# Layer 1 of a four-layer kernel: tiles 8 to 15 turned by crossbar DMA transposes, and the keys' map in one VectorE operation

## The chip, the cores and the metric

The kernel runs on one core of a Trainium2 chip. A core has five engines that work side by side, each through its own list of instructions in order: TensorE (PE in the profile; its weight loads, PEld, overlap its matmuls), VectorE (DVE), ScalarE (ACT), GpSimd (POOL) and SyncE (SP), which here issues the DMAs. An instruction that has to wait holds up all that stand behind it in its engine's list. The metric is the device time of one run in microseconds (us); less is better.

## The reference, cut to what matters

The input `A_x` has 2048 tokens (S) of 576 numbers (D). Four layers follow each other: linear attention, MLP, attention, MLP, with the same weights in both pairs. Each adds its result to x.

```python
def _A_ref(x, wqkv, wo):            # H = 32 heads of 18
    q, k, v = ...                   # (x @ wqkv), split by head
    phi = lambda t: jnp.where(t > 0, t + 1, jnp.exp(t)) + 1e-6
    pq, pk = phi(q), phi(k)
    kv = jnp.einsum("bhsd,bhse->bhde", pk, v)
    z = jnp.einsum("bhsd->bhd", pk)
    num = jnp.einsum("bhqd,bhde->bhqe", pq, kv)
    den = jnp.einsum("bhqd,bhd->bhq", pq, z)[..., None] + 1e-6
    return (num / den) @ wo         # heads joined again
def _B_ref(x, w1, b1, w2, b2):      # 576 -> 4608 -> 576
    h = _gelu(_layernorm(x) @ w1 + b1)
    return h @ w2 + b2
x = x + _A_ref(_layernorm(x), ...); x = x + _B_ref(x, ...)   # twice
```

## The kernel before, in words

Tokens are worked in 16 tiles of 128 rows (t = 0 to 15). Matmuls need the normalized rows y in turned form, features on partitions; this is `yT`, 5 blocks of 128 features (the fifth is only half full) by 2048 tokens.

The key phase of layer 1 is where the change lies. Per tile: the rows arrive by DMA in pairs (`load_x0`); `LNPipe.tick` takes them step by step through statistics (DVE, `bn_stats`), variance plus epsilon (`ln_u`), the reciprocal root (POOL, L433), mean times root (`nmr`, L436), and the normalization in place, by DVE for tiles 0 to 3 and by POOL for the others (L444). The last 64 columns of each row go to a separate ring, `v_ring`, with a column of ones behind them, so that a product with it also sums the keys. Then TensorE transposes the tile's five blocks into PSUM (L500) and ACT copies them into `yT` (L505).

`k_half` (L653) multiplies a tile of `yT` with half of the key weights, 288 columns, five matmuls per half. The map phi follows on PSUM: ACT makes the exponential; for the first half ACT makes k + 1 too and DVE takes min, add and max (`phi_from_psum`); for the second half DVE does the adding (`phi_by_dve`). `rows_by_keys` (L678) sums y^T times phi(k) over the tiles: four blocks into two accumulators (`k2_ps`), and a fifth product for the last 64 columns and the ones (`k_tail`). The values' weights come in later, on the sum (`kv_groups`). `q_proj` (L621) makes one group of the queries for 512 tokens.

The loop over t = 4 to 15 is written out: keys of tile t, one step of the pipe with the transposes of tile t + 1, a piece of late weights, masks on POOL, one query product, another step of the pipe, the sums of tile t. After the loop come two more query products, then the second half's ones and tails over all tiles (`last_rows_by_keys`, L707), then the second half's sums, woven with the rest of the attention.

What sets the order: a scheduler of the language orders instructions within an engine by its own estimate, but TensorE's list (`pe`), the start-up DMAs (`chained`) and the first operations of DVE and ACT (`in_order`) are tied by hand. SP's list carries x, the weights wqkv, and then one piece of w1, wo or w2 per turn of the loop (`late_pieces`); at most eight of its DMAs are under way, as each waits for the one eight places before it.

Layers 2 to 4 find their turned rows by another way (DVE transposes of 32 x 32 blocks and a trip through DRAM, `turn_rows` and `land`); layer 3 loads its rows back with `load_row` and the tails into `v_ring`.

Of the kernel before, what the change touches and what calls it, by code (L numbers as in the profile page):

```python
# [30 lines left out]
HALF = D // 2  # L31
LAST_PARTS = (slice(0, 3 * P), slice(3 * P, D))
# [3 lines left out]
def build(tc, A_x, A_wqkv, A_wo, B_w1, B_b1, B_w2, B_b2, out, dbg=None, n_layers=4):  # L36
    nc = tc.nc
    dbg = dbg or {}
    with ExitStack() as ctx:
# [107 lines left out]
        def row_tile(name):  # L147
            return rows.tile([P, D], F32, name=name, tag="row")

        x0_tiles = {}  # L150

# [32 lines left out]
        def load_x0(t):  # L184
            if t % 2 == 0:
                x0_tiles["pair"] = rows.tile([P, 2, D], BF16, name="x0", tag="row")
            x0 = x0_tiles["pair"][:, t % 2, :]
            chained(nc.sync.dma_start(out=x0, in_=x_in[t * P:(t + 1) * P, :]))
            x0_tiles[t] = x0
# [63 lines left out]
        def bias_casts():  # L253
            cast = nc.gpsimd.tensor_copy(out=b1T[:], in_=bias_stage.pop("b1")[:])
            tc.add_manual_dep(cast.ins, pool_last["norm"], NOSYNC, reason="bias is not urgent")
# [9 lines left out]

        def tail_of(t):

            flat = v_ring[t // 8][:].rearrange("p g c -> p (g c)")
            return flat[:, (t % 8) * 65:(t % 8 + 1) * 65]

        def tails(c):
            flat = v_ring[c // 2][:].rearrange("p g c -> p (g c)")
            return flat[:, (c % 2) * 260:(c % 2 + 1) * 260].rearrange("p (t e) -> p t e", e=65)

        def first_tail(t, width=65):

            slot = 2 * (t % 8) + t // 8
            flat = v_ring[slot // 8][:].rearrange("p g c -> p (g c)")
            return flat[:, (slot % 8) * 65:(slot % 8) * 65 + width]
# [9 lines left out]
        def load_row(t):  # L289
            if t % 2 == 0:  # L290
                pair = rows.tile([P, 2, D], BF16, name="yrow_pair", tag="row")
                row_of[t], row_of[t + 1] = pair[:, 0, :], pair[:, 1, :]
            load = nc.sync.dma_start(out=row_of[t][:, 0:4 * P], in_=yrow_d[t // TPC, t % TPC].rearrange("j r d -> (j r) d")[:, 0:4 * P])
# [22 lines left out]
        def land(now=False):  # L316

            for it in list(landing):
# [11 lines left out]
                if kind == "A":  # L330
                    if c == NCB - 1:
                        sp_last["landed"] = landed.ins.name
                    tail = nc.sync.dma_start(out=tails(c)[:, :, 0:64],
                                             in_=yrow_d[c].rearrange("i j r d -> (j r) i d")[:, :, 4 * P:D])
                    behind(tail, "landed")
# [11 lines left out]
        class LNPipe:  # L347
# [11 lines left out]
            def tick(self, transposes=1):  # L359
                land()  # L360
                for it in list(self.items):
                    st = it["stage"]
                    if st == 4 and it["evac"] != "dma":
# [12 lines left out]
                    elif st == 0 and it["stats"] == "act":  # L376
# [7 lines left out]
                        continue  # L384
                    elif st == 0.5:
# [4 lines left out]
                        nc.gpsimd.tensor_scalar(out=u[:], in0=mv[:, 1:2], scalar1=(1.0 + EPS) / D, scalar2=EPS * EPS,  # L390
# [48 lines left out]
                    elif st in (2, 3) and it["kind"] == "A" and it["evac"] == "act":  # L439
                        xt, t = it["xt"], it["t"]  # L440
                        tail = first_tail(t)[:, 0:64]
                        if it["norm"] == "pool":
                            for out, cols in ((xt[:, 0:4 * P], slice(0, 4 * P)), (tail, slice(4 * P, D))):
                                norm = nc.gpsimd.tensor_scalar(out=out, in0=xt[:, cols], scalar1=it["rstd"][:, 0:1],  # L444
                                                               scalar2=it["nmr"][:, 0:1], op0=ALU.mult, op1=ALU.add)
                            pool_last["norm"] = norm.ins.name
                        else:
                            for name, out, cols in ((f"n{t}", xt[:, 0:4 * P], slice(0, 4 * P)), (f"nt{t}", tail, slice(4 * P, D))):
                                norm = named(name, nc.vector.tensor_scalar(
                                    out=out, in0=xt[:, cols], scalar1=it["mv"][:, 0:1], scalar2=it["rstd"][:, 0:1],  # L450
                                    op0=ALU.subtract, op1=ALU.mult))
# [31 lines left out]
                    elif st == 4:  # L483
                        t = it["t"]
                        first_layer = it["kind"] == "A" and it["evac"] == "act"
                        y = it["xt"] if first_layer else it["y"]
                        if it["evac"] == "dma":
                            turn_rows(y, t, it["kind"])
                            self.items.remove(it)
# [8 lines left out]
                        for k in range(KD):  # L498
                            block = first_tail(t, P) if first_layer and k == 4 else y[:, k * P:(k + 1) * P]
                            pe(nc.tensor.transpose(out=(tp if k < 3 else tp2)[:, k, :], in_=block, identity=ident[:]))  # L500
# [34 lines left out]
        def phi_by_dve(ps_ap, out_ap, rows, n, tag=None):  # L535
# [8 lines left out]
            if tag is not None:  # L544
                named("e" + tag, exp), named("mi" + tag, low), named("ma" + tag, top)

# [68 lines left out]
        def layer_A(li, next_kind, pre_a1=None):  # L615
# [34 lines left out]
            def k_half(t, half, defer=False):  # L650
# [5 lines left out]
                by_dve = half or li == 0 and t == 2  # L656

                def phi():
                    if (half, t // 2) not in self_k["pk"]:
                        self_k["pk"][(half, t // 2)] = blk.tile([P, D], BF16, name="pk", tag="blk")  # L660
                    pk = self_k["pk"][(half, t // 2)][:, (t % 2) * HALF:(t % 2 + 1) * HALF]
                    (phi_by_dve if by_dve else phi_from_psum)(kp[:, 0:HALF], pk, P, HALF,
                                                              tag=f"{t}{half}" if li == 0 and t < 4 else None)
                if defer:
                    return phi
                phi()

            def rows_by_keys(t, half, chunks=(4, 0, 1, 2, 3), done=True):
# [5 lines left out]
                pk = self_k["pk"][(half, t // 2)][:, (t % 2) * HALF:(t % 2 + 1) * HALF]  # L674
                for k in chunks:
                    dst = self_k["tail"][0:65, 0:HALF] if k == 4 else self_k["acc"][k // 2][:, k % 2, 0:HALF]
                    lhsT = (tail_of(t) if li > 0 else first_tail(t)) if k == 4 else row_of[t][:, k * P:(k + 1) * P]
                    pe(nc.tensor.matmul(dst, lhsT=lhsT, rhs=pk, start=(t == 0), stop=(t == NT - 1)))  # L678
                cols = slice(half * HALF, (half + 1) * HALF)
                if 4 in chunks and t == NT - 1:  # L680
                    nc.gpsimd.memset(zk[:, cols], 0.0)
                    nc.scalar.copy(out=k2[4][0:64, cols], in_=self_k["tail"][0:64, 0:HALF])
                    nc.scalar.copy(out=zk[64:65, cols], in_=self_k["tail"][64:65, 0:HALF])
                if not done:
                    return
                if t % 2:
# [7 lines left out]
                for i, copy in enumerate((nc.scalar.copy, nc.vector.tensor_copy)):  # L694
# [518 lines left out]
```

## Time and profile before

| | |
|---|---|
| median of 3 runs | 760.14 us (760.12 to 760.39) |
| profiled execution, span from first to last instruction | 758.4 us |
| PE busy | 753.2 us, 99% of the span |
| PEld, ACT, DVE, POOL | 64%, 43%, 36%, 15% |
| granted TensorE clock | 1.000 |
| DMA | 73.90 MB, mean 97 GB/s |

The profile is of one execution. Its own time is given as the span, 758.4 us; the time of a run is taken outside it and has 1.74 us more in the median. A line of groups gives the source line, engine, operation, tiles (out<-in) and sizes, then the count, busy time and mean duration, and then the idle time before them. The chain of waits is followed back from the last instruction: start, duration and the work that set the time there. In the windows, each engine's busy time stands in a stretch of the span, then the granted clock, the DMA engines' mean share and GB/s.

### The profile page before, as it was taken

The numbers are of one execution on the slowest core, as the hardware profiler recorded it, in microseconds if no ns is written. First come the engines' busy times: TensorE is split into PE (matmuls) and PEld (weight loads), VectorE is DVE, ScalarE is ACT, GpSimd is POOL, SyncE is SP. The second block draws the span as 40 slices with busy tenths as digits, with TensorE's granted clock in tenths as the row PEclk, the third lists the DMA queues.
The fourth block names the chain that finished last, engine by engine and source line by source line (L and its number), as shares of the span: only waits on it lengthen the run. The fifth ranks groups of instructions, "written<-read, shape, count | busy, mean of one in ns | idle before, by whom it ended". The sixth has DMA issues, their size and how long they took to land.

```text
span 758.4 us, 15817 instructions
## 1 busy us (share of the span) xinstructions
PE 753.2 (99%) x6595; PEld 487.4 (64%) x6595; DVE 272.0 (36%) x685; ACT 328.7 (43%) x733; POOL 116.6 (15%) x196
## 2 busy tenths in 40 slices
PE   9999999999999999999999999999999999999998
PEld 5776754774477457646777777457646754774476
DVE  8876862136033503401367577600230131000000
ACT  6887656205600650263057666660174036205600
POOL 4840231002000301200100005300020020001000
PEclk9999999999999999999999999999999999999999
DMA  8994573026312711320404047530240033011000
GB/s 236 267 313 74 178 262 82 17 64 189 83 39 83 181 51 48 109 69 17 131 24 116 24 136 255 185 82 16 88 115 7 16 127 82 9 33 55 1 9 24
DMA packets 80977, 73.90 MB, mean 97 GB/s; under 512 B 36874, under 2 KB 65546, under 8 KB 80906
## 3 DMA queue, kind: packets, MB, share of 16 engines
q1 hardware_dynamic: 80906, 72.90, 33.0%
q8 instruction: 51, 0.84, 0.5%
q14 instruction: 20, 0.16, 0.1%
HBM read 48.10 MB, written 24.77 MB: 96 GB/s over the span
## 4 chain that ended last, share of the span: by engine, by line
PE 97%; DVE 1%; ACT 0%; issue 0%; DVEq 0%
PE m_ps L1104 36%; PE h_ps L1045 21%; PE hp_ps L1045 16%; PE q_ps L621 6%; PE k_ps L653 5%; PE wo_ps L933 5%; PE k_ps L678 4%; PE m_half L1104 1%; PE tp L500 1%; PE warm_ps L217 1%; PE k_tail L678 1%; PE kv_ps L719 0%; PE den_ps L769 0%; PE rden_ps L810 0%; PE kvwo_half L737 0%
## 5 line engine op out<-in xcount | busy, mean ns | idle before, releaser
L1104 PE MATMUL m_ps<-w_sb,hT 128*128 128x288 bf16 x2232 | 274.8, 286 | 0.0
L1104 PEld LDWEIGHTS <-hT 128*128 128x128 bf16 x2304 | 224.3, 98 | 60.4 <-issue 3.4
L1045 PEld LDWEIGHTS <-w_sb 64*128 64x128 bf16 x2304 | 124.5, 94 | 136.4 <-issue 1.9
L1045 PE MATMUL hp_ps<-yT,w_sb 64*128 64x512 bf16 x1152 | 178.0, 376 | 0.0
L1045 PE MATMUL h_ps<-yT,w_sb 64*128 64x512 bf16 x1152 | 148.0, 376 | 0.0
L1050 ACT COPY relay_sb<-relay_sb 128x1 f32<-128x1 f32 x144 | 28.5, 198 | 260.4 <-PE h_ps L1045 217.6
L1041 ACT ACTIVATE hT<-h_ps,b1T 128x512 bf16<-128x512 f32 x144 | 91.0, 683 | 44.1 <-PE h_ps L1045 44.1
L433 POOL TENSOR_TENSOR ln_rstd<-ln_u,neg_half 128x1 f32<-128x1 f32 x61 | 35.2, 577 | 439.9 <-DVE ln_u L415 218.0
L1041 ACT ACTIVATE hT<-hp_ps,b1T 128x512 bf16<-128x512 f32 x144 | 91.1, 692 | 0.0
L605 DVE TENSOR_TENSOR xbf<-m_ps,xo 128x576 bf16<-128x576 f32 x15 | 11.4, 757 | 213.5 <-PE m_ps L1104 213.5
L605 DVE TENSOR_TENSOR xo<-m_ps,xo 128x576 f32<-128x576 f32 x16 | 12.1, 757 | 172.6 <-PE m_ps L1104 172.6
L588 POOL TENSOR_TENSOR xo<-xo,b_bc 128x576 f32<-128x576 f32 x32 | 40.9, 1283 | 97.3 <-DMA xo<-x_d 58.4
L1045 PE MATMUL h_ps<-yT,w_tail 64*128 64x512 bf16 x144 | 54.1, 376 | 0.0
L1045 PE MATMUL hp_ps<-yT,w_tail 64*128 64x512 bf16 x144 | 54.1, 376 | 0.0
L621 PE MATMUL q_ps<-yT,wqkv_sb 128*126 128x512 bf16 (+1 forms) x200 | 49.3, 379 | 0.1
L653 PE MATMUL k_ps<-wqkv_sb,yT 128*128 128x288 bf16 x320 | 44.6, 286 | 0.2
L933 PE MATMUL wo_ps<-kvwo,pq 126*128 126x288 bf16 (+1 forms) x320 | 43.4, 286 | 0.3
L1045 PEld LDWEIGHTS <-w_tail 64*128 64x128 bf16 x288 | 27.1, 94 | 17.1
L653 PEld LDWEIGHTS <-yT 128*128 128x128 bf16 x320 | 31.0, 98 | 8.9 <-ACT yT L502 0.6
L933 PEld LDWEIGHTS <-pq 126*128 126x128 bf16 (+1 forms) x320 | 30.3, 97 | 9.1 <-issue 0.8
L621 PEld LDWEIGHTS <-wqkv_sb 128*126 128x126 bf16 (+1 forms) x200 | 25.7, 131 | 11.7 <-issue 0.5
L554 ACT ACTIVATE phi_e<-q_ps 126x512 bf16<-126x512 f32 (+1 forms) x40 | 23.9, 597 | 18.4 <-PE q_ps L621 16.8
(138 smaller groups left out, 591.6 us busy)
## 6 DMA issues: line engine op xcount, KB each, us to landing
xo<-x_d SPq DMA_DIRECT2D x48, 288.0 KB, 3.5
x_d<-xo SPq DMA_DIRECT2D x32, 288.0 KB, 2.6
xl<-x_d SPq DMA_DIRECT2D x24, 288.0 KB, 4.2
y_d<-turned SPq DMA_DIRECT2D x40, 144.0 KB, 3.1
w_sb<-in_B_w_dram SPq DMA_DIRECT2D x6, 864.0 KB, 10.4
yT<-y_d SPq DMA_DIRECT2D x10, 512.0 KB, 4.2
w_sb<-in_B_w_dram SPq DMA_DIRECT2D x9, 512.0 KB, 5.9
x_d<-xn SPq DMA_DIRECT2D x16, 288.0 KB, 3.3
```

Of the source, the lines that this page charges most:

```text
L433: nc.gpsimd.tensor_tensor(out=rstd[:], in0=it["u"][:], in1=neg_half[:], op=ALU.pow)
L554: exp = nc.scalar.activation(out=e_out, in_=ps_ap, func=ACT.Exp)
L588: nc.gpsimd.tensor_tensor(out=xo[:], in0=xo[:], in1=b2_bc[:], op=ALU.add)
L605: total = nc.vector.tensor_tensor(out=xn[:, cols].rearrange("p (h n) -> p h n", h=2), in0=halves, in1=xo[:, cols].rearrange("p (h n) -> p ...
L621: pe(nc.tensor.matmul(qp[0:GR[g], :], lhsT=wqkv_sb[:, k, GO[g]:GO[g] + GR[g]], rhs=yT[:, k, c * CA:(c + 1) * CA], start=(k == 0), stop=(k ...
L653: pe(nc.tensor.matmul(kp[:, 0:HALF], lhsT=yT[:, k, t * P:(t + 1) * P], rhs=wqkv_sb[:, k, D + half * HALF: D + (half + 1) * HALF], start=(k ...
L678: pe(nc.tensor.matmul(dst, lhsT=lhsT, rhs=pk, start=(t == 0), stop=(t == NT - 1)))
L933: pe(nc.tensor.matmul(wp[:, half, 0:HALF], lhsT=pq[(g, c)][0:GR[g], j * P:(j + 1) * P], rhs=kvwo[g][0:GR[g], half * HALF:(half + 1) * HALF ...
L1041: act_last["gelu"] = nc.scalar.activation(out=to, in_=ps, func=ACT.Gelu_apprx_tanh, bias=b1T[:, f:f + 1], scale=1.0).ins.name
L1045: mm = pe(nc.tensor.matmul(dst[n], lhsT=wt, rhs=mv, start=(seen[n] == 0), stop=(seen[n] == 8)))
L1050: relay = nc.scalar.copy(out=relay_sb[:, 1:2], in_=relay_sb[:, 0:1])
L1104: pe(nc.tensor.matmul(acc[half][:, 0:cols.stop - cols.start], lhsT=hT[f][:, j * P:(j + 1) * P], rhs=w2_sb[:, f, cols], start=(f == 0), sto ...
```

## The change

- Tiles 8 to 15 of layer 1 are no longer transposed on TensorE. SP issues one crossbar DMA transpose for each, from the 128 x 640 rows to the five blocks of `yT`. It stands in SP's list between the late weight pieces and waits for POOL's normalization.
- Row tiles are 640 wide (`RW`), their last 64 columns set to ones by POOL. The ring `v_ring`, the separate normalization of the last 64 columns, and layer 3's loads of tails go; the sums take the last columns and the ones from the row itself. `load_row` loads 576 columns, not 512.
- The weights' row that meets the first column of ones is set to 1 for the keys, so `k_half` yields k + 1. The map is then the exponential with bias -1 (ACT) and one DVE operation, min(max(k + 1, 1), e^k) (`phi_of_first`). The 1e-6 of phi is put in on the sums: a column of ones in the first half's keys (one POOL memset per tile) gives the rows' sums, DVE scales them (`key_eps`), and the copies of the accumulators add them (`plus_eps`).
- In the loop the sums of tile t - 1 stand ahead of the query product of turn t; after the loop a query product, the sums of tile 15, and the other query product.
- From turn 4 on, tiles are fed to the pipe four turns ahead, not three (turn 4 feeds two); tiles 9, 12 and 15 get their statistics from ACT.
- The 18 small loads of w1's tail rows become 2, after the main pieces; the last three pieces of w2 are issued in layer 1's output stage (t = 12 to 14).

```diff
+RW = DPAD
...
-        NV = 2
-        v_ring = [const.tile([P, G, P], BF16, name=f"v_ring{i}") for i in range(NV)]
+        key_eps = const.tile([P, 8], F32, name="key_eps")
         AHEAD = 4
+        XB = 8
...
-            return rows.tile([P, D], F32, name=name, tag="row")
+            return rows.tile([P, RW], F32, name=name, tag="row")[:, 0:D]
...
-        for vr in v_ring:
-            nc.gpsimd.memset(vr[:], 0.0)
-            nc.gpsimd.memset(vr[:].rearrange("p g c -> p (g c)")[:, 0:520].rearrange("p (t e) -> p t e", e=65)[:, :, 64:65], 1.0)
+        nc.gpsimd.memset(wqkv_sb[64:65, 4, D:2 * D], 1.0)
+        nc.gpsimd.memset(key_eps[:], 0.0)
+        nc.gpsimd.memset(key_eps[:, 6:7], 1e-6 * S / P)
+        for pair in x0_pairs:
+            nc.gpsimd.memset(pair[:, :, D:RW], 1.0)
...
-            ts = slice(i * 256, (i + 1) * 256)
-            for par in range(2):
-                chained(nc.sync.dma_start(
-                    out=w1_tail[64 * par:64 * (par + 1), ts].rearrange("k (f p) -> k f p", p=P),
-                    in_=B_w1[4 * P:D, cs].rearrange("k (f two p) -> k f two p", two=2, p=P)[:, :, par, :]))
+
+        def piece_w1_tail(par):
+            chained(nc.sync.dma_start(
+                out=w1_tail[64 * par:64 * (par + 1), :].rearrange("k (f p) -> k f p", p=P),
+                in_=B_w1[4 * P:D, :].rearrange("k (f two p) -> k f two p", two=2, p=P)[:, :, par, :]))
...
-                      [(lambda i=i: piece_w1(i)) for i in range(4, 9)] + [(lambda i=i: piece_w2(i)) for i in range(6)] + [piece_b1_dma]
+                      [(lambda i=i: piece_w1(i)) for i in range(4, 9)] + \
+                      [(lambda i=i: piece_w1_tail(i)) for i in range(2)] + [(lambda i=i: piece_w2(i)) for i in range(3)] + [piece_b1_dma]
+        last_pieces = [(lambda i=i: piece_w2(i)) for i in range(3, 6)]
...
-                pair = rows.tile([P, 2, D], BF16, name="yrow_pair", tag="row")
+                pair = rows.tile([P, 2, RW], BF16, name="yrow_pair", tag="row")
+                nc.gpsimd.memset(pair[:, :, D:RW], 1.0)
...
-                            for out, cols in ((xt[:, 0:4 * P], slice(0, 4 * P)), (tail, slice(4 * P, D))):
-                                norm = nc.gpsimd.tensor_scalar(out=out, in0=xt[:, cols], scalar1=it["rstd"][:, 0:1],
-                                                               scalar2=it["nmr"][:, 0:1], op0=ALU.mult, op1=ALU.add)
+                            norm = nc.gpsimd.tensor_scalar(out=xt[:, 0:D], in0=xt[:, 0:D], scalar1=it["rstd"][:, 0:1],
+                                                           scalar2=it["nmr"][:, 0:1], op0=ALU.mult, op1=ALU.add)
...
+                        if it["evac"] == "xbar":
+                            chained(nc.sync.dma_start_transpose(out=yT[:, :, t * P:(t + 1) * P], in_=y[:, 0:DPAD]))
+                            self.items.remove(it)
+                            continue
...
+        def phi_of_first(ps_ap, out_ap, n, tag=None):
+            e = exp_tile(tag)[:, 0:n]
+            exp = nc.scalar.activation(out=e, in_=ps_ap, func=ACT.Exp, bias=-1.0)
+            act_last["exp"] = exp.ins.name
+            top = nc.vector.scalar_tensor_tensor(out=out_ap, in0=ps_ap, scalar=1.0, in1=e, op0=ALU.max, op1=ALU.min)
+            dve_last["phi"] = top.ins.name
...
+                    if li == 0 and half == 0:
+                        pk = self_k["pk"][(0, t)] = blk.tile([P, D], BF16, name="pk", tag="blk")
+                        pool_last["pk"] = nc.gpsimd.memset(pk[:, HALF:HALF + 1], 1.0).ins.name
+                        phi_of_first(kp[:, 0:HALF], pk[:, 0:HALF], HALF, tag=f"{t}0" if t < 4 else None)
+                        return
...
+                summed = li == 0 and half == 0
+                n = HALF + summed
...
+                if summed and t == NT - 1:
+                    for i in range(2):
+                        nc.vector.tensor_scalar(out=key_eps[:, 2 * i:2 * i + 2].unsqueeze(2),
+                                                in0=self_k["acc"][i][:, :, HALF:HALF + 1], scalar1=1e-6, scalar2=None,
+                                                op0=ALU.mult)
...
-                for i, copy in enumerate((nc.scalar.copy, nc.vector.tensor_copy)):
+                for i, engine in enumerate((nc.scalar, nc.vector)):
                     for j in range(2):
-                        copy(out=k2[2 * i + j][:, cols], in_=self_k["acc"][i][:, j, 0:HALF])
+                        plus_eps(engine, k2[2 * i + j][:, cols], self_k["acc"][i][:, j, 0:HALF],
+                                 key_eps[:, 2 * i + j:2 * i + j + 1])
...
+                    if t > 4:
+                        rows_by_keys(t - 1, 0)
                     q_proj(*q_left.pop(0), defer=True)(after=act_last["turned"])
                     lnp.tick(transposes=0)
-                    rows_by_keys(t, 0)
-                for _ in range(2):
-                    q_proj(*q_left.pop(0))
+                q_proj(*q_left.pop(0))
+                rows_by_keys(NT - 1, 0)
+                q_proj(*q_left.pop(0))
...
+                if last_pieces and t >= NT - TPC:
+                    last_pieces.pop(0)()
...
         def feed0(t, after=None):
-            lnp.feed(x0_tiles.pop(t), t, "A", l0_norm_eng(t), "act", after=after)
+            lnp.feed(x0_tiles.pop(t), t, "A", l0_norm_eng(t), "act" if t < XB else "xbar", after=after,
+                     stats="act" if t >= XB and t % 3 == 0 else "dve")
...
-            if t + 3 < NT:
-                feed0(t + 3, after=dve_last["phi"])
+            for ahead in (3, 4) if t == 4 else (4,):
+                if t + ahead < NT:
+                    feed0(t + ahead, after=dve_last["phi"])
```

More of the change, by code (lines that the diff above doesn't have):

```diff
@@ L185, in load_x0 @@
             if t % 2 == 0:
[L186 removed]
+                x0_tiles["pair"] = rows.tile([P, 2, RW], BF16, name="x0", tag="row")
             x0 = x0_tiles["pair"][:, t % 2, :]
[L188 removed]
+            chained(nc.sync.dma_start(out=x0[:, 0:D], in_=x_in[t * P:(t + 1) * P, :]))
+            if t % 2 == 0:
+                x0_pairs.append(x0_tiles["pair"])
             x0_tiles[t] = x0
@@ L666, in k_half, with plus_eps @@
                 phi()
+            def plus_eps(engine, out, in_, eps):
+                if li > 0:
+                    (engine.copy if engine is nc.scalar else engine.tensor_copy)(out=out, in_=in_)
+                elif engine is nc.scalar:
+                    engine.activation(out=out, in_=in_, func=ACT.Identity, bias=eps)
+                else:
+                    engine.tensor_scalar(out=out, in0=in_, scalar1=eps, scalar2=None, op0=ALU.add)
             def rows_by_keys(t, half, chunks=(4, 0, 1, 2, 3), done=True):
@@ L1075, in run @@
                 for c in range(NCB):
+                    if c == 2 and next_kind == "A":
+                        zero = nc.gpsimd.memset(wqkv_sb[64:P, 4, D:2 * D], 0.0)
+                        tc.add_manual_dep(zero.ins, act_last["gelu"], NOSYNC, reason="not urgent")
                     for g in range(self.done.get(c, 0), NGRP):
```

88 lines of the change are left out of this document (43 added, 45 removed).

## The prediction

> **What bounds the kernel now.** I read the page's busy shares first, then the chain of waits, then the windows over the loop that the change touches.
>
> ```profile
> span 758.4 us, 15817 instructions
> PE 753.2 (99%) x6595; PEld 487.4 (64%) x6595; DVE 272.0 (36%) x685; ACT 328.7 (43%) x733; POOL 116.6 (15%) x196
> PE 97%; DVE 1%; ACT 0%; issue 0%; DVEq 0%
> ```
>
> TensorE (PE) is busy 753.2 of 758.4 us and is 97% of the chain. So what leaves TensorE's list shortens the run, as long as nothing makes it wait instead. The share of an engine over the span says little of the touched loop; the window from tile 4's keys to tile 15's query product does:
>
> ```profile
> 18.07:55.28 37.21, 37.21 (x287) 27.92 (x285) 31.40 (x109) 30.82 (x70) 25.43 (x57) 1.00 0.99 284
> ```
>
> In these 37.21 us PE is busy throughout, DVE 84%, ACT 83%, POOL 68%, the 16 DMA engines 99% at 284 GB/s, and the granted clock is 1.00. One turn of the loop in the chain:
>
> ```profile
> 27.87 1.23 PE k_ps L653 x10
> 29.09 0.28 PE tp L500 x5
> 29.37 1.15 PE q_ps L621 x5
> 30.52 0.19 PE k_tail L678
> 30.71 0.49 PE k_ps L678 x4
> 31.20 1.23 PE k_ps L653 x10
> ```
>
> Most turns take 3.26 us: keys, five transposes of the next tile, a query product, five sums. Of these 0.28 us are the transposes.
>
> **The change part by part.**
>
> *TensorE transposes of tiles 8 to 15 go.* 8 x 0.28 = 2.24 us off a chain that is all PE: -2.24. The eight ACT copies (687 ns each) were hidden under PE and are worth nothing by themselves. The 80 sums of the first half get a 289th column: a 288-column matmul runs 0.123 us (1.23/10), so 80 x 0.123/288 = +0.03.
>
> *The start.* Before 12 us the DVE sits on the chain. In the timeline PE's fourth tile transpose begins at 12.01, though the keys before it (from 10.44, 1.23 us) end at 11.67; it waited for the tail normalization that ends at 11.59 and the key map that follows. The change takes out the separate tail normalizations (0.2 us of DVE each) and the min-and-add passes (0.14 to 0.23 each), and turns two maps of 0.30 into maps from PSUM of 0.46. I book the gap, 0.34, plus nothing more, as the other gaps wait for ACT copies or for weights that stay: -0.35, bounds -0.6 to 0.
>
> *ACT and DVE in the loop.* A key map falls from exp, identity, min-and-add, max to exp and one DVE operation. ACT loses an identity (0.41) and, from tile 8, a copy (0.69); it gains two statistics passes on tiles 9, 12 and 15, at most 0.69 each by the 640-column copy. The fullest turn (tile 5) then has a copy 0.6, two exps 0.6, two query passes 1.0 and the passes 1.1, 3.3 us at the pace at which ACT issues, against 3.26 for PE; the next turn has 2.2. So at most a tenth of a us, which I leave at nothing. DVE gets lighter. If that cover were gone, the price would be the 1.1 us of the passes, three times.
>
> *POOL.* Normalizations of 512 and 64 columns become one of 576. From these rows of tile 8
>
> ```profile
> 25.16 0.83 POOL L433 TENSOR_TENSOR ln_rstd<-ln_u,neg_half 128x1 f32<-128x1 f32 x1 [0.17 <-ACT phi_a L555]
> 26.10 0.37 POOL L436 TENSOR_SCALAR ln_nmr<-ln_mv,ln_rstd 128x1 f32<-128x1 f32 x1
> 26.57 0.77 POOL L444 TENSOR_SCALAR x<-x,ln_rstd,ln_nmr 128x512 bf16<-128x512 bf16 x1
> 27.32 0.40 POOL L444 TENSOR_SCALAR v_ring<-x,ln_rstd,ln_nmr 128x64 bf16<-128x64 bf16 x1
> ```
>
> a tile takes 2.51 us start to end; without the tail's 0.35 and with 0.05 for 64 columns more it takes 2.2, and tile 9's rows give 1.9. I use 1.95, nearer to tile 9 because DVE, whose operations POOL's run beside, has fewer; 0.3 more where ACT made the statistics. Masks add 0.6 per turn in most turns to tile 12, and a one-column memset of each key map 0.1. These memsets are a new wait: the sums of a tile now wait for POOL. In the changed instruction order the memset of tile 6's map stands behind the normalization of tile 9 and its masks. Tile 7's variance is there at 21.6 (DVE's timeline, before and, with 0.35 less ahead and tile 8's statistics mixed in, after). Then tile 8's normalization ends at 25.6, tile 9's at 28.4, the memset at 29.1. The sums of tile 6 would start at 28.1: with 0.35 gained at the start, turn 4 without its sums (-0.61) and turn 7 without transposes, keys 5, 6, 7, 8 stand at 20.35, 23.6, 26.9 and 29.85, and the sums follow keys 7 by 1.23. Bounds 0 to 1.0 us; the later memsets come in time. I take the middle: +0.5. Before the change no sum waits for POOL, so this cannot be a gain.
>
> *The crossbar transposes.* Eight DMAs of 128 x 640 bf16, 160 KB, are issued by SP, each behind POOL's normalization. Behind the waiting transpose stand all weight pieces that follow it in SP's queue; the 18 small tail pieces are folded into 2, behind the main pieces, and three w2 pieces go to the output stage. First, the deadline. Tile 8 may be issued at 25.6 and its keys start at 29.85, so it has 4.2 us to land; tile 15, ready at about 44.5, has 6 to its keys at 50.7. From 25.6 to 50.7 the queue carries, in the changed instruction order, eight transposes, six main pieces of 512 KB and wo of 648 KB. At the window's 284 GB/s a piece takes 1.85 us and wo 2.34, 13.4 together, so a transpose may hold the queue for (25.1 - 13.4)/8 = 1.46 us before keys wait. The price of one is not in the trace; the nearest row has the same kind of source and about the same bytes, in 256-byte pieces:
>
> ```profile
> y_d<-turned SPq DMA_DIRECT2D x40, 144.0 KB, 3.1
> 120.19 2.46 SPq L310 DMA_DIRECT2D y_d<-turned  x4
> 125.19 0.39 SPq L325 DMA_DIRECT2D yT<-y_d  x1
> ```
>
> (the first line from the DMA issues, the others from SP's timeline). One lands in 3.1; four, issued together, are all landed 5.0 us after the first, 1.25 each. For 160 KB that is 1.39, just under the limit, and a lone one lands in 3.1 of its 4.2 us. The far row is the 9 KB load of b1 in 2-byte pieces: 4608 of them keep SP 2.31 us, and a transpose element by element would have 81,920, 41 us. I take the near row because source, bytes and partitions agree: +0. Lower bound 0 too, since the saving is booked above; upper bound 8 x 41.
>
> [...]
>
> *Later stages.* The end of the key phase: the sums of tile 15 now have one query product (1.08) less between them and the second half's sums, which reuse their accumulators: 1.08 + 0.60 + 1.10 = 2.78 us of PE cover. The copies end about 2.1 after the sums (query pass 0.6, key_eps 0.2 to 0.5, four ACT copies 1.3): hidden, +0; without cover up to 0.5. Weights: w1 and its tails end near 55 us and are wanted at 101.8; three w2 pieces (864 KB, about 3 us each) are issued from some 93 us, wanted from 141. Layer 3's wider row loads and their POOL memsets replace tail loads, against rows that are there some 8 us early: nothing.
>
> **Sum** on the profiled execution: -2.24 + 0.03 - 0.35 + 0.5 = -2.06, 758.4 to 756.3 of span. The median of 760.14 is 1.74 above that span, so 758.1.
>
> **The rivals.**
> (1) Late once. The five 128 x 128 blocks of a tile are turned one after the other, each at the 1.25 us of a y_d store, but tiles overlap. One lands 6.25 us after its issue, tile 8 at 31.85 instead of 29.85, a stall of 2.0; the rest keep pace. For it: weight pieces land after 5.9 us when the queue is full. Against: the queue drains while SP waits for POOL. Time 758.1 + 2.0 = 760.1, no change. [...]
> (2) The other sign: the DMA queue becomes the bound. If a transpose holds the queue for its 3.1 us of landing, the eighth lands at 25.6 + 8 x 3.1 + 13.4 = 63.8, 13.1 us after its keys were due: 771.2. With five blocks in turn, 6.25 each, it is 38.3: 796. It begins at 1.46 us and eats the gain of 2.06 at 1.72. For it: 99% DMA share in the loop and SP's strict order. Against: the change takes 16 small DMAs out of that stretch.
> (3) The crossbar is hidden and POOL's memsets are early: 758.1 - 0.5 = 757.6, and with 0.3 more at the start 757.3.
>
> **How the numbers follow.** Forecast with (3), whose span of times is 757.0 to 759.0: 0.58. Rival (1): 0.19. Rival (2): 0.23, half of it above 767. A measurement of this kernel tells 0.2%, 1.5 us, from no change. Faster takes nearly all of the first case, 0.57; no change (1) and the rest, 0.20; slower (2), 0.23. The range goes from 757.0 to 767, leaving some 0.05 below and 0.12 above.
>
> **What would show it.** In the changed profile: turns of 2.98 us in the chain from tile 7 on, no wait of PE's weight loads of yT for a DMA, transposes landing in 2 to 4 us, the memset's wait at PE of at most 1 us near 28 us, the second half's sums without a gap. It would be wrong if keys 8 to 15 wait for a DMA by more each tile (2), by about 2 us once (1), or if SP's issue of a transpose takes over 2 us.

## The result and the profile after

The changed kernel takes 758.65 us (median of 16 runs, 758.32 to 759.67), the kernel before 760.13 us in the same series (16 runs, 760.02 to 760.57). The ratio is 0.9981, with a 95% interval of 0.9975 to 0.9988: 1.48 us less, where the sum had 2.06. The changed kernel's times spread more than those of the kernel before.

The page of the changed kernel, first its busy shares, then the chain that ended last:

```profile
span 757.2 us, 15677 instructions
PE 750.6 (99%) x6555; PEld 484.7 (64%) x6555; DVE 261.3 (35%) x641; ACT 323.3 (43%) x722; POOL 114.9 (15%) x219
PE 95%; DMA 1%; ACT 1%; DVE 1%; POOL 1%; SPq 0%; issue 0%; POOLq 0%; DVEq 0%
```

PE has 40 instructions less, the transposes of eight tiles, and is still the chain. But its share of the chain fell from 97 to 95%, and DMA, ACT, DVE and POOL have about 1% each: the run waits for others where it did not before. This execution took 759.16 us, 0.5 above the median. The spans of all runs have a median of 756.75.

The windows of the changed kernel from tile 4's keys to the end of tile 15's (length; busy time and count of PE, PEld, DVE, ACT and POOL; granted clock, DMA share and GB/s):

```profile
18.30:53.12 34.82, 34.21 (x243) 24.83 (x241) 24.02 (x75) 25.39 (x63) 21.04 (x60) 1.00 0.89 208
```

The stretch is 2.4 us shorter than the one of before. PE is no longer busy throughout (0.61 us idle), and DVE and ACT have 7 and 5 us less to do. One steady turn in its chain (the last five lines), and ahead of it the place where POOL's fill of a key map, the one-column memset, comes in:

```profile
28.32 1.23 PE k_ps L657 x10
29.55 0.24 PE k_tail L699
...
34.29 1.23 PE k_ps L657 x10
35.51 0.12 PE k_tail L699
35.63 0.49 PE k_ps L699 x4
36.13 1.08 PE q_ps L625 x5
37.21 1.23 PE k_ps L657 x10
```

A steady turn is now 2.92 us, all of it PE, against 3.26. In turn 7 the first sum starts 0.12 us late (0.24 for 0.12): that is the whole price of the fill. PE's waits from 8 to 60 us and, from PE's timeline, the first of them:

```profile
PE tp L494 <- DVE x L440: 0.6, 1, 0.6
PE q_ps L625 <- DVE pk L546: 0.4, 1, 0.4
PE tp L494 <- ACT phi_a L559: 0.2, 1, 0.2
```

```profile
9.61 0.45 PE L494 MATMUL tp<-ident,x 128*128 128x128 bf16 x5 [0.62 <-DVE x L440]
```

Three waits, none of them for a DMA, and none of them in the profile before (that one has a single wait here, the 0.18 us at tile 3's transposes). SP's timeline, where the crossbar transposes are issued:

```profile
25.94 1.33 SPq L483 DMA_TRANSPOSE yT<-x  x1
27.32 0.57 SPq L237 DMA_DIRECT2D w_sb<-in_B_w_dram  x1
28.88 1.21 SPq L483 DMA_TRANSPOSE yT<-x  x1
```

An issue took SP 1.21 to 1.39 us for these eight, against 0.57 to 0.58 for a weight piece among them. The page gives no landing times for these DMAs; the experiments below do.

Where the time went, by the starts in PE's timeline of the kernel before, of the changed kernel and of its second profile (the run "again" below):

| start of | before | after | again |
|---|---|---|---|
| keys of tile 4 | 17.91 | 18.14 | 18.00 |
| keys of tile 8 | 31.04 | 31.20 | 31.08 |
| keys of tile 15 | 53.89 | 51.65 | 51.53 |
| last tails of layer 1 (z_rows) | 59.06 | 57.44 | 57.32 |
| layer 2 (h_ps) | 101.74 | 100.14 | 100.89 |
| layer 3, keys | 383.48 | 381.87 | 382.62 |
| layer 4 (h_ps) | 473.56 | 472.46 | 472.94 |

The start loses 0.1 to 0.2 us. Turns 4 to 7 are a draw (13.13 us before, 13.06 after), although 0.61 us of sums left turn 4 and 0.28 us of transposes left turn 7. From tile 8 to 15 the loop gains 2.40 us. From tile 15's keys on the 0.61 us of sums come back. At the end of layer 1's key phase 1.62 to 1.74 us are won. The rest of the program runs as before, except two output stages, which in these two profiles together give back 0.5 and 1.1 us.

### The profile page after: what moved, and what is told of

Read it like the earlier page. It is cut to its first block, busy times and chain, and to the rows that moved or that the text cites. A ratio compares the mean times of both kernels' runs of the same rounds, so it can differ in the third digit from the quotient of the medians.

```text
span 757.2 us, 15677 instructions
## 1 busy us (share of the span) xinstructions
PE 750.6 (99%) x6555; PEld 484.7 (64%) x6555; DVE 261.3 (35%) x641; ACT 323.3 (43%) x722; POOL 114.9 (15%) x219
## 4 chain that ended last, share of the span: by engine, by line
PE 95%; DMA 1%; ACT 1%; DVE 1%; POOL 1%; SPq 0%; issue 0%; POOLq 0%; DVEq 0%
PE m_ps L1144 36%; PE h_ps L1082 21%; PE hp_ps L1082 16%; PE q_ps L625 5%; PE k_ps L657 5%; PE k_ps L699 4%; PE wo_ps L968 3%; PE m_half L1144 1%; DMA xo<-x_d 1%; DMA x<-in_A_x_dram 1%; PE k_tail L699 0%; PE kv_ps L751 0%; ACT turned L846 0%; PE rden_ps L842 0%; PE den_ps L801 0%
## 5 line engine op out<-in xcount | busy, mean ns | idle before, releaser
L609 DVE TENSOR_TENSOR xo<-m_ps,xo 128x576 f32<-128x576 f32 x16 | 12.1, 757 | 168.2 <-PE m_ps L1144 168.2
```

The costliest lines, as they stand in the source:

```text
L609: total = nc.vector.tensor_tensor(out=xn[:, cols].rearrange("p (h n) -> p h n", h=2), in0=halves, in1=xo[:, cols].rearrange("p (h n) -> p ...
```

## The experiments

All times are medians in us; the kernel before stood at 760.35, 760.42 and 760.37 in the three series.

**The changed kernel again.** No edit.

> The changed kernel once more. The first profile of it lost 0.23 us by the start of tile 4's keys (18.14 us against 17.91 before), with the statistics of tile 3 waiting 0.64 us for that tile's load, and 0.5 us in layer 3, where TensorE waits 0.4 us for the sum of a residual row whose load landed late (wo_ps at 471.14 us). Theory: both depend on when a load happens to land. Then a second profile has tile 4's keys elsewhere, between 17.6 and 18.2 us, and layer 3's wait missing or of another size, with a span between 756.0 and 757.2 us, and the median of the times stays at 758.3 to 759.0 us. Rival: both belong to the changed order. Then both stand in the second profile at the same places, within 0.1 us, and the span is 757.2 us again.

Measured: 758.96 (12 runs, 758.66 to 762.07), ratio 0.9987 (0.9979 to 0.9995); the profiled run 759.6, span 757.7. Neither theory holds whole, and the span is above the range of the first. The loop is the same within 0.02 us a turn: the lost time of turns 4 to 7 is regular. Tile 4's keys stand at 18.00, and in the ten profiles of this text whose kernels leave the start alone they stand anywhere from 17.75 to 18.14, with a mean of 17.9, the place of before. The waits of the output stages do move. In layer 3 the wait for the residual row is gone, and one of 0.41 us for POOL stands in its place. In layer 1, in DVE's timeline, a store of a row had not landed:

```profile
90.37 0.76 DVE L609 TENSOR_TENSOR xn<-wo_ps,xo_pair 128x576 f32<-128x576 f32 x1 [0.97 <-DMA x_d<-xn]
```

**All tiles by TensorE**, the rest of the change kept (the condition on the statistics still names tile 8).

```diff
-        XB = 8
+        XB = 16
```

> All sixteen tiles turned by TensorE, the rest of the change kept. Theory: the crossbar is what shortens the loop. The steady turn goes from 2.93 us back to 3.27, 8 turns by 0.34 = 2.7 us, so 761.3 us, above the kernel before (760.1), because what the first profile lost at the start and in turns 4 to 7 stays. Rival A: the turns got shorter by the new order of sums and query products: a turn of 2.93 to 3.0 us stays and the time is 758.6 to 759.2. Rival B: by my predicted price of five transposes, 0.28: 760.9.

Measured: 762.32, ratio 1.0027 (1.0017 to 1.0037). The crossbar is what shortens the loop: without it the change loses 2 us against the kernel before. The keys of tiles 8 to 15 start 3.31 us apart, 0.39 more than with the crossbar, and two turns take 3.77 and 3.57, with these two waits of PE in its waits from 30 to 58 us (first row, the sum of both):

```profile
PE tp L494 <- ACT phi_a L559: 0.6, 2, 0.4
```

They are the turns in which ACT makes the statistics, and the copies of the transposed tiles are back on it: from 31.36 to 58.15 us ACT is busy for 20.51 us, 77%, against 16.19 us, 69%, from 31.20 to 54.57 in the changed kernel. So 761.3 was 1.0 too low: the two parts of the change need each other, ACT's passes the copies that the crossbar saves.

**The sums back in their own turn.**

```diff
-                    if t > 4:
-                        rows_by_keys(t - 1, 0)
                     q_proj(*q_left.pop(0), defer=True)(after=act_last["turned"])
                     lnp.tick(transposes=0)
-                q_proj(*q_left.pop(0))
-                rows_by_keys(NT - 1, 0)
+                    rows_by_keys(t, 0)
+                q_proj(*q_left.pop(0))
```

> Every tile's sums back in the tile's own turn, behind the query product, as in the kernel before; crossbar and one-operation map kept. Theory: the one-column fill of each key map stands on GpSimd behind the normalization of a tile three turns ahead; tile 6's fill ends at 29.4 us, and with the old order its sums would be wanted some 2.3 us after tile 6's keys begin at 24.6, that is at 26.9: a stall of 2.5 us, once, and smaller ones in the turns behind it. At the end of the key phase 1.1 us of cover go, with the copies ending 2.1 us after the sums and 1.7 us of TensorE work ahead of the next sums: 0.4 us. Together 761.5 us. Rival: GpSimd's fill is early enough there too, and the order of sums and query products is worth nothing: 758.4 to 759.1 us.

Measured: 760.86, ratio 1.0006 (0.9997 to 1.0015), 1.9 above the changed kernel beside it. PE's waits from 20 to 60 us:

```profile
PE k_tail L699 <- POOL pk L663: 1.3, 2, 0.8
PE q_ps L625 <- DVE pk L546: 0.9, 2, 0.5
```

The fill of the key map is late, twice, at 29.31 and 39.01 us; the chain there runs through POOL's normalizations. The stall is smaller than the 2.5 us that I expected for tile 6, but comes twice. So without the new place of the sums nothing is left of the gain. PE has nothing less to do by it; it gives POOL and DVE the time of the next tile's keys, 1.23 us.

**Two transposes for each tile**, one into a region that nobody reads.

```diff
-                            chained(nc.sync.dma_start_transpose(out=yT[:, :, t * P:(t + 1) * P], in_=y[:, 0:DPAD]))
+                            spare = w2_sb[:, 32 + 2 * (t % 2):34 + 2 * (t % 2), :].rearrange("p a b -> p (a b)")
+                            for out in (spare[:, 0:DPAD].rearrange("p (k n) -> p k n", k=KD), yT[:, :, t * P:(t + 1) * P]):
+                                chained(nc.sync.dma_start_transpose(out=out, in_=y[:, 0:DPAD]))
```

> Each of tiles 8 to 15 is turned twice by the crossbar, first into a spare region that nobody reads and then into its place; nothing else changed. It prices the crossbar on the queue. Theory of the prediction: a transpose holds the queue about as long as a store of the same bytes in 256-byte pieces, 1.25 to 1.39 us. A turn then asks the queue for a weight piece (1.85 us) and two transposes (2.8 us), 4.6 us against 2.93 of TensorE: 1.7 us in each of 7 turns, less the 2.4 us of head start that the first one has: 768 us, with TensorE waiting for yT in the later tiles. Rival A: a transpose costs its bytes only, 0.56 us at 284 GB/s; then the turn asks for 2.97 us, and the time is 758.6 to 759.2 us. Rival B: SyncE's issue of 1.2 to 1.4 us each is the cost: 2 x 1.21 + 0.58 = 3.0 us a turn, 759.3 us. Rival C: five blocks one after the other, 6.25 us each: over 800 us.

Measured: 763.09 (4 runs), ratio 1.0039 (1.0025 to 1.0054), 4.1 above the changed kernel. That is half of what my price said, and more than the bytes. SP's timeline:

```profile
40.71 1.21 SPq L485 DMA_TRANSPOSE w_sb<-x  x1
41.97 1.33 SPq L485 DMA_TRANSPOSE yT<-x  x1
43.34 0.59 SPq L237 DMA_DIRECT2D w_sb<-in_B_w_dram  x1
44.04 1.27 SPq L485 DMA_TRANSPOSE w_sb<-x  x1
```

SP issues without a pause, 3.33 us a turn against PE's 2.92. So SyncE's issue is the limit: rival B has the mechanism (8 turns by 0.41 is 3.3 of the 4.1), but its 3.0 us a turn and 759.3 us were too low. The rest is not taken apart. In 3.33 us the queue also took a weight piece, 1.85 us at the 284 GB/s of before, and it did not fall behind: in the chain the transpose issued at 33.59 us landed after 5.33 us, the last, issued at 51.93, after 3.84. So I estimate that a transpose holds the queue for at most (3.33 - 1.85)/2 = 0.74 us, not for the 1.25 to 1.39 that I took.

**Tile 2's normalization earlier on DVE**, and **the statistics of tiles 9, 12 and 15 on DVE**, alone and together.

```diff
-g2 cd1 s3a ma00 n2 s3b
+g2 cd1 n2 s3a ma00 s3b
```

```diff
-                     stats="act" if t >= XB and t % 3 == 0 else "dve")
+                     stats="dve")
```

> Tile 2's normalization (DVE, 0.42 us) placed ahead of tile 3's first statistics and tile 0's key map in DVE's hand-written order; nothing else changed. In both profiles of the changed kernel DVE stands idle until 8.26 to 8.39 us for tile 3's load, then does statistics and map, and TensorE waits 0.33 to 0.62 us at tile 2's transposes for the normalization, whose scale is ready at 8.34. Theory: this order is what turned my predicted gain of 0.35 at the start into a loss; the wait goes, tile 4's keys begin 0.3 to 0.6 us earlier (17.5 to 17.7 us), the time is 758.1 to 758.5 us. Rival: the work after it is bound elsewhere (the map of tile 0 or tile 3's normalization becomes late in its place), tile 4's keys stay at 17.9 to 18.1 us, and the time stays at 758.6 to 759.0 us.

> The statistics of tiles 9, 12 and 15 on DVE instead of two accumulating passes on ScalarE. I had costed these passes at nothing. Theory: with their read-outs (0.21 us each, not in my sum) they make ScalarE late in turn 5, where two key maps, a copy, a query map and the passes stand from 22.3 to 26.0 us; without them the 0.22 us wait of tile 7's transposes and the stretched keys of tile 6 go, turn 6 falls from 3.6 to 3.3 us, and the time falls by 0.3 us to 758.3 to 758.7 us. Rival: the 1.2 us that each of the three tiles adds to DVE stands ahead of key maps there and costs as much: 758.7 to 759.5 us, with waits of TensorE for DVE's pk in their place.

> Both edits together: tile 2's normalization earlier, and the statistics of tiles 9, 12 and 15 on DVE. Theory: they are separate stretches of one TensorE chain and add: 757.7 to 758.3 us. Rival: starting turn 4 earlier only makes TensorE wait longer in turns 5 to 7, for DVE or GpSimd, whose chain of statistics runs by its own clock: then no better than the better one of the two alone.

Measured: 758.78, 759.12 and 759.26, ratios 0.9979 (0.9970 to 0.9988), 0.9988 (0.9979 to 0.9997) and 0.9988 (0.9978 to 0.9997). None beats the changed kernel by more than these intervals. With the normalization earlier the wait at tile 2's transposes goes, but PE waits 0.27 us at tile 1's keys for DVE's map (pk) instead, and tile 4's keys start at 17.85, within the spread of the others: the rival. With the statistics on DVE, ACT's wait goes and turns 6 and 7 fall from 3.58 and 3.05 to 3.51 and 2.92; the second is the stall for POOL's fill, which comes earlier because POOL need not follow ACT's passes. So the passes cost 0.2 us of the loop, not the 0.3 that I expected here and not the nothing of the prediction. The time did not fall by it: 759.12 is in the rival's range, though the waits for pk that the rival named are not there. In the profiled run it is layer 3's output stage that gives the gain back (25.19 us against 24.41 before). Together the edits failed in an instructive way. Chain and PE's timeline of the run with both:

```profile
33.62 0.83 POOL x L436
34.45 0.03 POOL head_sel L72
34.47 5.73 DMA yT<-x
```

```profile
40.25 1.40 PE L657 MATMUL k_ps<-wqkv_sb,yT 128*128 128x288 bf16 x10 [0.43 <-DMA yT<-x]
```

Tile 11's transpose took 5.73 us from issue to landing, and its keys came 0.59 us late. The gain of the two edits ran into the crossbar.

**Tiles 6 and 7 by the crossbar too** (statistics as they were).

```diff
-        XB = 8
+        XB = 6
```

> Tiles 6 and 7 by the crossbar too (statistics by ScalarE still for tiles 9, 12, 15). Theory: two more turns lose their transposes (0.34 us each) and ScalarE two copies of 0.69 us in the turns where it is late (0.3 us): 757.7 to 758.0 us. Rival: tile 6's normalization ends at 20.8 us; the run with doubled transposes showed landings of 4.0 to 5.3 us after the issue when the queue was loaded, so tile 6 would be there at 24.8 to 26.1 us, against its keys at 24.5 us or earlier: TensorE waits 0.5 to 1.5 us for yT once, and the time is 758.3 to 759.3 us.

Measured: 759.76, ratio 0.9990 (0.9982 to 0.9999): 0.8 above the changed kernel's second series, though the two intervals overlap. The trace shows the rival, one tile later than I put it. Turn 5 falls to 2.92. Tile 6, issued at 20.77, is in time for keys at 23.94, so it landed within 3.2 us. Tile 7, issued at 23.88, is not, and behind it POOL's fill is late as well:

```profile
27.98 1.40 PE L657 MATMUL k_ps<-wqkv_sb,yT 128*128 128x288 bf16 x10 [0.96 <-DMA yT<-x]
29.66 0.28 PE L699 MATMUL k_tail<-pk,x 128*65 128x289 bf16 x1 [0.27 <-POOL pk L663]
```

**No weight pieces among the transposes** but one behind the first, on the kernel with both edits (the diff leaves those two out).

```diff
-            if late_pieces:
+            if late_pieces and t < 7:
                 late_pieces.pop(0)()
```

> The two edits together (tile 2's normalization earlier, statistics on DVE), and no weight piece issued between the transposes: w1's pieces 3 to 8, wo and the rest follow the last transpose. With both edits alone tile 11's keys waited 0.43 us for a transpose that took 5.73 us from issue to landing, and 4 of 12 times lay above 759.5 us. Theory: it is the weight pieces on the queue that stretch a transpose's landing from about 3.2 us (tile 6's, in the run with tiles 6 and 7 turned by the crossbar) to 5.7, and now and then beyond the 5.2 us that there are. Then no keys wait, every turn from tile 8 on is 2.92 us, SyncE issues each transpose in 1.21 us, no time lies above 759.5, and the median is 758.2 to 758.7 us. Rival A: the landing is the crossbar's own and varies by itself: waits for yT stay, and the times spread as before. Rival B: the weights, now all behind the loop, delay the residual rows of the output stage, and the time rises above 759.3 us with a wait there.

Measured: 762.11 (759.96 to 763.97), ratio 1.0020 (1.0010 to 1.0029). In the loop the theory holds: PE waits for no transpose, every turn from tile 7 on is 2.92 us, and layer 1's tails start at 56.90, the earliest of all. The total goes by rival B. The weights, all behind the loop now, push the residual rows back: SP begins with their loads at 69.18 us, against 58.13 in the changed kernel. PE's timeline:

```profile
81.22 1.39 PE L968 MATMUL wo_ps<-kvwo,pq 126*128 126x288 bf16 x10 [2.40 <-DVE xn L609]
```

The wait cost more than its own 2.40 us. After it the granted clock was 0.74 from 81.2 to 84.0 us and 0.68 from there to 87.0, where the run with both edits has 1.00. That is an estimated 1.7 us more (2.8 x 0.26 + 3.0 x 0.32), and the stretch from the tails to layer 2 took 46.61 us against 42.76. So the spread of the times could not be tested this way; it got larger (759.96 to 763.97), which the new wait may explain.

**The landing time**: each tile turned twice into the same place, with and without the weight pieces between.

```diff
-                            chained(nc.sync.dma_start_transpose(out=yT[:, :, t * P:(t + 1) * P], in_=y[:, 0:DPAD]))
+                            for _ in range(2):
+                                chained(nc.sync.dma_start_transpose(out=yT[:, :, t * P:(t + 1) * P], in_=y[:, 0:DPAD]))
```

> Each of tiles 8 to 15 is turned twice into the same place, so the second transpose waits on SyncE until the first has landed: SyncE's timeline then shows the landing time of the first, with weight pieces ahead of it on the queue. By my prediction it is 3.1 us (2 to 4); then SyncE needs 6.2 + 0.6 us a tile, the keys' turns become 6.8 us, and the time is some 784 us. Rival: 4 to 5.7 us, as the waits of the other runs say: turns of 9 to 12 us and 800 to 825 us. Five blocks one after the other at 1.25 us each would be 6.25 us.

> The same doubling with no weight piece between the transposes: the landing of a lone transpose on an empty queue. Theory: 3 to 3.3 us, well below the loaded queue's, and a time at least 10 us below that of the run with the pieces between. Rival: the landing is the same as in that run within 0.3 us, so that it belongs to the crossbar and not to the queue.

Measured, one run each: 783.14 and 776.80. SP's second transpose waits for the first to land (eight waits of SP for a transpose's DMA, 22.8 us in the first run and 12.1 in the second), so the time between the two starts is the landing. First with the weight pieces, then without:

```profile
36.70 1.21 SPq L484 DMA_TRANSPOSE yT<-x  x1
41.08 1.20 SPq L484 DMA_TRANSPOSE yT<-x  x1
...
43.48 1.20 SPq L484 DMA_TRANSPOSE yT<-x  x1
48.59 1.20 SPq L484 DMA_TRANSPOSE yT<-x  x1
```

```profile
40.25 1.23 SPq L484 DMA_TRANSPOSE yT<-x  x1
42.92 1.20 SPq L484 DMA_TRANSPOSE yT<-x  x1
44.21 1.23 SPq L484 DMA_TRANSPOSE yT<-x  x1
46.83 1.20 SPq L484 DMA_TRANSPOSE yT<-x  x1
```

A transpose behind a weight piece landed after 4.0 to 5.1 us in seven tiles of the first run. With no weight piece ahead it landed after 2.6 to 2.8 us, in seven of the eight tiles of the second run and in the first tile of the first; the second run's tile 9, behind its only weight piece, took 4.73. In most of these tiles the second transpose of the tile before had been issued only 1.3 us earlier, so in these runs it is the weight piece ahead that makes the difference, not a transpose ahead. Theory's 3 to 3.3 us was a little high. The first run's time agrees with 784 by accident: I had two landings of 3.1 us in each turn, and it is one of 4.4 and one issue of 1.2. The second run's tails of layer 1 start 14.7 us earlier, but its late weights give 8.5 of that back by layer 2 (6.0 of it one wait for a residual row), so its total is 6.3 us lower, not 10.

**Five DMAs for each tile.**

```diff
-                            chained(nc.sync.dma_start_transpose(out=yT[:, :, t * P:(t + 1) * P], in_=y[:, 0:DPAD]))
+                            for k in range(KD):
+                                chained(nc.sync.dma_start_transpose(out=yT[:, k, t * P:(t + 1) * P],
+                                                                    in_=y[:, k * P:(k + 1) * P]))
```

> Each tile's 128 x 640 transpose cut into five DMAs of 128 x 128. It tells what SyncE's 1.21 us of issue consists of. If it goes by the data (five blocks of 0.24 us), the five take 1.2 to 1.5 us, a turn asks SyncE for 2 us, and the time stays within 1 us of 758.8. If it is paid for each DMA, the five take 6.05 us, a turn asks SyncE for 6.7 us against 2.92, and the time is 758.8 + 8 x 3.8 - 3 (head start), about 786 us. My first rival's five blocks turned one after the other, tiles overlapping, would show as landings of 6 us with little change in SyncE's issue.

Measured, one run: 791.34, 5 us above the 786 of the theory that it is paid for each DMA. SP's timeline has one row for a tile:

```profile
54.62 6.20 SPq L484 DMA_TRANSPOSE yT<-x  x5
```

1.24 us each, against 1.21 for the whole 128 x 640 tile in the changed kernel: here SyncE's issue went by the DMA, not by its bytes. What made the other 5 us is not taken apart.

## Why the prediction was right, and where its steps failed

The sign and the likeliest case came out. Of the predicted 2.06 us of span, 1.55 came by the second series (median spans 758.6 and 757.05) and 1.65 by the first (758.4 in the profiled run of before, a median of 756.75 after). Another 0.17 us went outside the span: the changed kernel's times lie 1.90 us above their spans, those of the kernel before 1.73. That part is not explained; it is there without the crossbar too (1.89 with all tiles by TensorE).

*Transposes, -2.24.* Too small: 2.40 us in the seven turns from tile 8 to 15, 0.34 each, not 0.28 (the eighth tile's lie in turn 7). The row of five transposes was not their whole cost: the query product behind them takes 1.08 us in the chain now and took 1.15, so 0.07 of the product's row was theirs.

*The 289th column, +0.03.* Too small to be seen.

*The start, -0.35.* This step failed. The gap that it named did close (tile 2's keys to tile 3's fell from 2.83 to 2.49 us), but "plus nothing more" was wrong: tile 0's keys to tile 1's took 3.0 to 3.5 us against 2.83 in nearly all profiles. DVE, relieved of the tail normalization and the min-and-add passes, reaches tile 3's statistics earlier, waits for that tile's load (0.64 us in the first profile), and keeps map and normalization behind it. Net: nothing, in the mean over ten profiles.

*ACT and DVE in the loop, nothing.* Failed. ACT's passes cost 0.2 us of the loop; each has a read-out of 0.21 to 0.23 us that I had left out. "DVE gets lighter" misled more: turn 4 takes 3.13 us, not 2.65, with 0.39 of wait at the query product for DVE's key map in every profile. The map now reads PSUM on DVE alone, behind a tile's statistics, where ACT's two passes freed half of the buffers before. That this is the reason is argued from the chain (query map, statistics, key map, query product); no run took it apart.

*POOL, +0.5.* Its times were right (1.84 to 1.94 us for the three tiles from 22.16 us on, where I took 1.95; that DVE's lighter load is the reason is not shown), the fill at 29.36 us against 29.1, but PE was 1.4 us behind my plan (tile 7's keys at 28.32 us in the chain against 26.9), so the stall was 0.12 and rival (3), in which it is none, was right about the fill and not about the time. When the sums are put back, the full price appears: 1.3 us of waits.

Turns 4 to 7 together took 13.06 us, where the plan's keys had 12.1 (17.7 to 29.85) and the stall another 0.5: 0.4 more than planned. DVE's map, ACT's passes and the fill account for 0.7 of the 0.9 above the keys alone; turn 6 takes 3.51 us even with the statistics on DVE, and why is open.

*The crossbar, +0.* Right in the sum, right for a lone landing (2.7 against 3.1), right that rival (2) does not come: PE waits for no transpose in either profile of the changed kernel. The reason was half wrong. By the estimate above a transpose holds the queue for at most 0.74 us, and with two for each tile SP's issue bound, at 3.33 us a turn. What decides is the landing behind a weight piece, 4.0 to 5.7 us, outside the 2 to 4 that I gave as a sign of being right. In the changed kernel tiles 8 to 15 have 5.2 to 5.9 us from issue to keys, partly because PE is late, and that is luck: tile 9, issued at 28.88 us with a weight piece ahead, would have had 4.0 us to its keys by my plan (29.85 + 2.98). Rival (1) is therefore nearer than it looks: two small improvements of the loop or two more tiles are enough to meet it, 0.6 to 1.1 us once.

On rival (1): it has five blocks in turn at 1.25 us each, so 6.25 for a tile. The whole tile in one DMA landed in 2.6 to 2.8 us with no weight piece ahead, less than the 3.1 of the store. As five DMAs its blocks took SyncE 1.24 us each to issue; how soon a single block lands was not measured.

*End of the key phase, +0.* Right: no gap ahead of the second half's sums.

*Later stages, nothing.* Nearly right for the median span. But in the two profiles layer 3's output stage took 24.92 and 24.65 us, from its first output product to layer 4, against 24.41, and once layer 1's lost 0.9 us to a store. The 24.92 are a residual row's load. The 24.65 are POOL: its copy of 64 columns took 0.83 us there instead of 0.30, and PE waited 0.41 for it. That wait stands in ten of the thirteen profiles of the changed kernel and its variants and not in the one of the kernel before, so it may be a regular cost of 0.24 us; one profile of before cannot tell. The waits for DMAs differ from run to run, and with transposes that are now and then late they may make the wider spread. What sets them off stays open.

That the sum came within half a us is in part luck: by my estimate the transposes' greater worth (8 x 0.34 = 2.7, not 2.24) and the cheaper fill (0.12, not 0.5) made up for 0.8 of the 1.4 us that the start, turns 4 to 6 and layer 3 cost beyond the plan.

## What to carry to other kernels

Work taken off the bounding engine is worth the change of the whole turn, not the row of the removed instructions (here 0.34 us, not 0.28); read it from the neighbours' rows too. An engine that gets less to do is not earlier everywhere: ask which buffer it now frees alone, and which load it will meet sooner (here tile 3's, a wait of 0.64 us). A transfer that hides only because something else is late will be the next bound: here one crossbar transpose in one DMA cost its issuing queue 1.2 us, and it landed 2.6 to 2.8 us after its start with no weight piece ahead and 4.0 to 5.1 behind one. A stall of the bounding engine can cost more than its length: look at the granted clock behind it (here 0.74 and 0.68 for 5.8 us behind a wait of 2.40, an estimated 1.7 us).

## What the runs showed of the hardware

- SyncE mostly needed 1.2 to 1.3 us to issue a crossbar transpose, of 128 x 128 as of 128 x 640, against 0.57 to 0.58 for a 512 KB weight piece between them in the changed kernel; one block took 1.99 (five DMAs for each tile).
- In the runs that turned each tile twice, the 128 x 640 transpose landed 2.6 to 2.8 us after its start with no weight piece ahead and 4.0 to 5.1 behind one; with both edits tile 11's took 5.73.
- Behind the two accumulating passes of ScalarE over 576 columns (0.69 and 0.81 us from 22.73 and 24.26 us in the changed kernel) stands an instruction of 0.21 and 0.23 us, ACTIVATION_READ_ACCUMULATOR in the trace.
- After some long waits of TensorE the granted clock was low: 0.74 and then 0.68 for 5.8 us after a wait of 2.4 us (no weight pieces), 0.50 for 2.6 us after waits of 3.4 and 4.4 us (each tile turned twice), where the ten key matmuls behind took 2.58 us. After 3.6 us in the run without weight pieces between it stayed at 1.00, and those ten took 1.40. What decides is not shown.
